# Windowed attention and two mixings on one core: one normalisation per attention tile, fourteen casts on GpSimd, another beginning and end

## The chip, the core and the metric

One NeuronCore of a Trainium2 chip runs one program. TensorE (PE) multiplies matrices, VectorE (DVE), ScalarE (ACT) and GpSimd (POOL) work on tiles of 128 partitions, SyncE (SP) issues nearly all DMAs. The metric is the device time of one execution in microseconds; smaller is better. Before the change it is 547.12 us, the median of 3 runs (547.0 to 549.04).

## The reference

```python
scores = scale * q @ k.T + bias            # 2 batches, 8 heads, 768 rows, head size 64
keep = is_global | is_local                # the first n_global columns, and a band of n_local
a = softmax(where(keep, scores, -1e9));  x = a @ v          # joined to [2, 768, 512]
xn = (x - mean) / sqrt(var + 1e-6) * g_ln
x = x + relu(xn @ w_ch1) @ w_ch2           # first mixing, 512 -> 2048 -> 512
u = x + (relu(x.T @ w_tok1) @ w_tok2).T    # token mixing, 768 -> 256 -> 768
out = u + relu(u @ moe2_w_ch1) @ moe2_w_ch2      # second mixing, 512 -> 1536 -> 512
```

The weights are float64 in DRAM and are read as 64-bit words. With these inputs n_global is 8 and n_local is 96, so a row tile of 128 attends to its own and the previous column tile.

## The kernel before, in words

The 1536 rows are 12 tiles T of 128. `window_tile` writes the attention of one tile: for two pairs of heads at a time the scores (L451, PE), the mask with the row maximum (L468, DVE), the exponential (L473, ACT), the transposed probabilities (L478, PE), their copy out of PSUM (L526 on ACT or L529 on DVE), the product with V (L483, PE), and at the end the division by the row sums (`scale`, L537 to L539, DVE). The product has a 65th column of ones, so the row sum comes out of the same matmul. Tiles 0 to 5 work in float32 this way; tiles 6 to 11 split the probabilities into two halves of 16 bits and transpose them on PE or by a DMA (the string `PT`).

`norm_ops` normalises a tile: statistics (L609 to L611, DVE), a power and two products (L618 to L621, POOL), the scaling (L624, ACT), the gain (L631, POOL), a high half (L587, ACT), a low half (L589, DVE or POOL), and a transposing DMA into `xa` or `xb` (L591, SP). Three tiles make a group; a mixing's first matmul needs all three.

`Weights.split` makes a weight block of 128 x 512 from a staged 512 KB load (`stg`, L166): a cast of the top words to float16 (`fw`, L755, ACT), a join with the shifted bits (`wf`, L761, DVE), the high half (L777, ACT), the low half (L780 POOL or L783 DVE). The first mixing has 16 blocks `a` and 16 blocks `b`. `mm3` (L372 to L374) multiplies halves in three products.

The program of each engine is written out by `Plan`: every step is an `Op` with an engine, a cost and a priority, and `order` picks, engine by engine, the ready step of the least priority whose buffers are free. The priorities come from the tables at the foot (`AHEAD`, `SLOT`, `LEADS` and others), the engine of many steps from strings of letters (`V` DVE, `G` POOL, `A` ACT). Between the steps of the beginning `emit` puts matmuls without use (`keep_busy`, L106), which keep PE's clock from falling.

PSUM is four pools of two banks: `m`, `s`, `t` and `k`. Before the change pool `t` holds both the transposed probabilities and the products with V (`PV`); pool `k` is used by `chain`, the accumulators of the mixings' paired products, from 236 us on.

`setup_consts` runs first: two tiny DMAs bring n_global and n_local to one partition (L50), DVE turns them into floats (L80, L83) and the flag that picks the fast path (L93 to L95), a matmul with a row of ones spreads the values over 128 partitions (L87), and a copy brings them out of PSUM (L97). Then the masks. At the end, tiles 10 and 11 are stored after the plan's other steps, both on SP (L1119), then every engine reads the flag `again` (L1437) and jumps over the general path (L1439).

Of the kernel before, what the change touches and what calls it, by code (L numbers as in the profile page):

```python
# [44 lines left out]
def setup_consts(o, tp):  # L45

    tc, nc, cp = o.tc, o.nc, o.cp
    w = tp.tile([1, 2, 2], I32, name="nwords")
    for i, n in enumerate((o.n_global, o.n_local)):
        (nc.sync, nc.scalar)[i].dma_start(w[:, i, :], n.bitcast(I32).rearrange("(o a) -> o a", o=1))  # L50
    for x in FIRST:
        if len(x) == 2:
            load(o, x[1], x[0])
        elif o.w64:
            load_words(o, o.stgs[len(o.staged)], x)
            o.staged.append(x)
# [3 lines left out]
    ones = tp.tile([1, P], F32, name="ones")  # L60
    nc.vector.memset(ones[:], 1.0)
    idle = o.nps.tile([P, 256], F32, name="idle")
    keep_busy(o, idle, BUSY[0])
# [12 lines left out]
    for fw in o.fws:  # L76
        nc.scalar.memzero(fw[:])

    neg = tp.tile([1, 2, 1], F32, name="neg")
    nc.vector.scalar_tensor_tensor(out=neg[:], in0=w[:, :, 0:1], scalar=0.0, in1=w[:, :, 1:2], op0=ALU.is_lt,  # L80
                                   op1=ALU.add)
    nval = tp.tile([1, 2, 1], F32, name="nval")
# [9 lines left out]
    ng, nl = nval[:, 0, :], nval[:, 1, :]  # L92
# [16 lines left out]
def distances(o, tp):  # L109


    nc = o.nc
    ri = tp.tile([P, 4 * P], I32, name="ri")
    ci = tp.tile([P, 1, NGF], I32, name="ci")
    rel = o.cp.tile([P, 4 * P], F32, name="rel")
    col = o.x[NTT - 2][:, :NGF].rearrange("p (o c) -> p o c", o=1)
    t = tp.tile([P, 4 * P], F32, name="mt")
# [7 lines left out]
    nc.vector.tensor_tensor(out=rel[:], in0=rel[:], in1=t[:], op=ALU.max)  # L125
    return rel, col
# [250 lines left out]
def bank(o, use, *dims):  # L377

    t = o.ps[BANKS[use]].tile([P, 512], F32, tag=BANKS[use], name=use)
# [20 lines left out]
def window_tile(o, plan, prio, T, slot):  # L400
# [33 lines left out]
    if T >= SPLIT:  # L434

        ao = Buf("ao", lambda: o.sm.tile([P, H, 2, D + 1], F32, tag="ao", name="ao", bufs=2))
        sm = Buf("sum", lambda: o.sm.tile([P, H], F32, tag="sum", name="sum", bufs=3))
    mn = Buf("mn", lambda: o.sm.tile([P, H], F32, tag="mn", name="mn", bufs=3))
    x = o.x[T][:].rearrange("p (h d) -> p h d", h=H)
    for p in range(4):  # L440
        k = k0 + p
        if p % 2 == 0:
# [12 lines left out]
            if T < SPLIT:  # L455
                bv = psum_buf(o, "PV", [4, D + 1])
# [4 lines left out]
        if T >= SPLIT:  # L461
            pt = Buf("ph", lambda: o.sm.tile([P, 8, P], F16, tag="ph", name="ph", bufs=o.sizes["ph"]))
            pq = Buf("pq", lambda: o.sm.tile([P, 8 * P], F16, tag="pq", name="pq", bufs=o.sizes["pq"]))
            bv = psum_buf(o, "PV", [2, 2, D + 1])
# [15 lines left out]
        def pv(p=p, pt=pt, bv=bv):  # L480
# [50 lines left out]
        if T < SPLIT:  # L531
            op("T", 2 * PVC * n, prio(k + slot["PV"]), pv, r=[(pt, 0), *vkeys], w=[(bv, p % 2)], get=[bv] if p % 2 == 0 else [])
        if T < SPLIT and p % 2 == 1:
            sm = Buf("sum", lambda: o.sm.tile([P, 4], F32, tag="sum", name="sum", bufs=3))

            def scale(p=p, bv=bv, sm=sm):
                nc.vector.tensor_scalar(out=sm.t[:], in0=bv.t[:, :, D], scalar1=1e-9, scalar2=None, op0=ALU.add)  # L537
                nc.vector.reciprocal(out=sm.t[:], in_=sm.t[:])
                nc.vector.tensor_tensor(out=x[:, 2 * p - 2:2 * p + 2], in0=bv.t[:, :, :D], in1=sm.t[:].rearrange(  # L539
                    "p (h o) -> p h o", o=1).to_broadcast([P, 4, D]), op=ALU.mult)  # L540

            op("V", 0.7, prio(k + slot["inv"]), scale, r=[(bv, 0), (bv, 1)], w=[("x", T, p // 2)], get=[sm])
# [101 lines left out]
class Guard:  # L644
# [7 lines left out]
    def __init__(self, o, plan):  # L652
# [7 lines left out]
        o.junk = o.gp.tile([P, 512], BF16, name="junk")  # L660
        for k, (a, b, lo, hi) in self.AT.items():
            for i, y in ((1, lo), (2, hi)):
                plan.op("G", 0.2, GUARD0, lambda i=i, a=a, b=b, y=y: nc.gpsimd.memset(c[:, i, a:b], y), w=[("lim", k, i)])
        for i, y in enumerate((1.0, TINY)):
            plan.op("G", 0.2, GUARD0, lambda i=i, y=y: nc.gpsimd.memset(o.ones[:, i:i + 1], y), w=[("one", i)])
# [48 lines left out]
class Weights:  # L714
# [26 lines left out]
    def split(self, src, prio, dst, key, get=(), r=(), after=()):  # L741
# [360 lines left out]
PVE = 'VAAAAV'  # L1102
EVX = 'AAAAVVAAVAVA'
QKC, PVC = 0.266, 0.224
SLOT = {'gk': -109.0, 'exp': 30.58, 'T': -47.76, 'PV': -30.42, 'inv': 2.16, 'st': 2.77, 'xn': 23.42, 'tr': 35.01}
NACT = range(0, 4)
START = {"V": 1.1, "A": 1.5, "G": 3.5, "S": 9.0}
# [3 lines left out]
BANKS = {'L1': 'm', 'L2': 'm', 'L2S': 't', 'norm': 'k', 'chain': 'k', 'uT': 't', 'S': 's', 'T': 't', 'PV': 't', 'tok1': 's', 'tok2': 't'}  # L1111
# [5 lines left out]
def store(o, T):  # L1117
    b, t = divmod(T, NT)
    o.nc.sync.dma_start(o.out[b, t * P:(t + 1) * P, :], o.x[T][:])  # L1119


def rest_pools(o, ctx):
# [15 lines left out]
    o.ps = {p: pool("ps" + p, o.sizes[p], space=PSUM) for p in PSUMS}  # L1138
# [3 lines left out]
def rest(o, ctx, attn, fast):  # L1142
# [136 lines left out]
LEADS, FLEAD = 25.19, 159.37  # L1279
F2LEAD = [-28.4, -27.06]  # L1280
FE, SE = 'VGVVVVGVVGVG', 'GVGGVVVV'
HEAD = 56.45
DUE = [32.72, 16.66, 78.81, 48.03]
EARLY = [42.85, -26.35, 1.23, -4.64]
LEAD = -178.69
EVAC = 20.66
TOK1 = 41.8
TOKW, TOK0 = 247.08, 102.37
# [5 lines left out]
class WindowAttention:  # L1294
# [8 lines left out]
    def ops(self, o, plan, prio):  # L1303
# [3 lines left out]
        plan.op("G", 0.3, 20.0, lambda: nc.gpsimd.memset(o.vb[:, :, :, 0, D:], VSC), w=[("vb", z, 0) for z in range(3)])  # L1307
        plan.op("G", 0.5, 20.0, lambda: nc.gpsimd.memset(o.vb[:, :, :, 1, D:], 0.0), w=[("vb", z, 1) for z in range(3)])
        plan.op("V", 1.25, HEAD0 + 8.0, lambda: may(o, o.bmt, o.col, o.x[NTT - 1][:, :3 * P], 0, 3, False), r=[("first", 1, 1)], w=[("rel",)], lock=True)
# [17 lines left out]
class GeneralAttention:  # L1327
# [7 lines left out]
    def attend(self, o, ctx):  # L1335
# [16 lines left out]
        for T in range(NTT):  # L1352
# [24 lines left out]
            for h in range(H):  # L1377
# [16 lines left out]
                acc = bank(o, "PV", 512)  # L1394
# [15 lines left out]
def mixer_kernel(ctx, tc, q, k, v, n_global, n_local, g_ln, w1, w2, wt1, wt2, w3, w4, out):  # L1410
# [20 lines left out]
    near = nc.values_load(flag[0:1, 0:1], min_val=0, max_val=1)  # L1431
# [5 lines left out]
    again = nc.values_load(o.again[0:1, 0:1], min_val=0, max_val=1)  # L1437
# [50 lines left out]
```

## Time and profile before

| | before |
|---|---|
| median of 3 runs | 547.12 us |
| the profiled execution's own time | 546.87 us |
| its span, first to last instruction | 545.1 us |
| mean granted TensorE clock | 0.996 of 2.4 GHz |
| PE, DVE, ACT, POOL busy | 532.0, 408.6, 337.1, 163.2 us |
| DMA moved | 89.81 MB, 57.2% of 16 engines' span |

Some 1.8 us of an execution lie outside the span. A busy PE counts matmuls without use too, and matmuls overlap, so the question is not how busy PE is but when its needed work may start and where it then stops.

### The profile page before, as it was taken

The page shows a single profiled execution, that of the slowest core. Times are in us where ns is not written, and L with a number is a line of the kernel's source. Part 1 is how long each engine was busy: PE and PEld are TensorE (multiplying, and loading weights), DVE is VectorE, ACT ScalarE, POOL GpSimd, SP SyncE. Part 2 cuts the span into 40 slices and gives each one's busy share as a digit, 9 for nine tenths or more (in the row PEclk, how much of TensorE's full clock was granted, in tenths as well). Part 3 has the DMA queues.
Part 4 walks back from the last instruction along what each step waited for, and adds up shares of the span by engine and source line. Part 5 has one row for each costly group of instructions (what it writes and reads, how often), then busy time and mean ns, then how long its engine had stood idle before and what let it go on. Part 6 is the DMA issues. An engine that isn't in the chain of part 4 may idle for free.

```text
span 545.1 us, 9103 instructions
## 1 busy us (share of the span) xinstructions
PE 532.0 (98%) x3132; PEld 299.7 (55%) x3132; DVE 408.6 (75%) x902; ACT 337.1 (62%) x760; POOL 163.2 (30%) x181
## 2 busy tenths in 40 slices
PE   7989999999999999999999999999999999999995
PEld 5866666666555555555555555455445545555542
DVE  6977998788699632788897898988987786655341
ACT  6988668786976433459948766576685545524210
POOL 2133221223132424253444245324343442220000
PEclk9998999999999999999999999999999999999999
DMA  8898977695998568277319793146745332302012
GB/s 242 267 232 238 294 209 182 202 259 164 208 234 237 207 174 231 97 240 244 97 39 192 186 267 110 40 136 210 268 121 158 92 133 68 113 1 78 2 40 82
DMA packets 99242, 89.81 MB, mean 165 GB/s; under 512 B 58484, under 2 KB 72820, under 8 KB 99188
## 3 DMA queue, kind: packets, MB, share of 16 engines
q1 hardware_dynamic: 99186, 89.15, 57.2%
q8 instruction: 26, 0.43, 0.3%
q14 instruction: 28, 0.23, 0.1%
q10 hardware_dynamic: 2, 0.00, 0.0%
HBM read 61.87 MB, written 17.83 MB: 146 GB/s over the span
## 4 chain that ended last, share of the span: by engine, by line
PE 84%; ACT 6%; DVE 4%; DMA 2%; SPq 1%; issue 1%; POOL 0%; ACTq 0%
PE L L372 11%; PE L L374 11%; PE L L373 11%; PE L2S L372 9%; PE L2S L374 9%; PE L2S L373 9%; PE chain L372 4%; PE chain L374 4%; PE chain L373 4%; PE S L451 3%; DMA stg<-in_moe_w_ch_dram 2%; PE tok L373 2%; PE tok L372 2%; PE tok L374 2%; ACT ex L473 2%; PE T L478 2%
## 5 line engine op out<-in xcount | busy, mean ns | idle before, releaser
L372 PE MATMUL L2S<-wb,h 128*128 128x512 f16 x228 | 86.4, 379 | 0.0
L373 PE MATMUL L2S<-wb,h 128*128 128x512 f16 x228 | 86.4, 379 | 0.0
L374 PE MATMUL L2S<-wb,h 128*128 128x512 f16 x228 | 86.4, 379 | 0.0
L900 DVE SCALAR_TENSOR_TENSOR x<-L2S,x 128x512 f32<-128x512 f32 x57 | 39.2, 688 | 43.0 <-PE L2S L374 42.9
L755 ACT ACTIVATE fw<-stg 128x512 f16<-128x512 bf16 x62 | 47.5, 777 | 20.1 <-DMA stg<-in_moe_w_ch_dram 16.2
L374 PEld LDWEIGHTS <-h 128*128 128x128 f16 x336 | 32.9, 98 | 39.6
L372 PEld LDWEIGHTS <-h 128*128 128x128 f16 x336 | 33.1, 98 | 35.7
L373 PEld LDWEIGHTS <-h 128*128 128x128 f16 x336 | 32.9, 98 | 35.8
L834 POOL TENSOR_TENSOR Q<-wa 128x512 f32<-128x512 f16 x18 | 25.6, 1422 | 74.8 <-DVE sz L834 55.2
L473 ACT ACTIVATE ex<-ex,mn 128x256 f32<-128x256 f32 (+1 forms) x96 | 41.3, 480 | 7.5 <-DVE mn L468 7.4
L761 DVE SCALAR_TENSOR_TENSOR wf<-stg,fw 128x512 uint32<-128x512 uint32 x62 | 45.0, 739 | 0.5 <-ACT fw L755 0.5
L834 POOL TENSOR_TENSOR Q<-Q 128x256 f32<-128x256 f32 x36 | 31.5, 874 | 32.6 <-DVE Q L834 31.2
L372 PE MATMUL L<-wb,h 128*128 128x512 f16 x108 | 40.9, 379 | 0.0
L373 PE MATMUL L<-wb,h 128*128 128x512 f16 x108 | 40.9, 379 | 0.0
L374 PE MATMUL L<-wb,h 128*128 128x512 f16 x108 | 40.9, 379 | 0.0
L372 PEld LDWEIGHTS <-wa 128*128 128x128 f16 x268 | 26.2, 98 | 20.4 <-issue 2.7
L374 PEld LDWEIGHTS <-wa 128*128 128x128 f16 x268 | 26.2, 98 | 17.3
L373 PEld LDWEIGHTS <-wa 128*128 128x128 f16 x268 | 26.2, 98 | 17.3
L364 DVE SCALAR_TENSOR_TENSOR h<-L,h 128x384 f16<-128x384 f32 x40 | 22.1, 553 | 17.4 <-ACT h L358 17.1
L372 PE MATMUL L<-xa,wa 128*128 128x384 f16 x104 | 34.0, 327 | 0.0
L373 PE MATMUL L<-xa,wa 128*128 128x384 f16 x104 | 33.9, 326 | 0.0
L374 PE MATMUL L<-xa,wa 128*128 128x384 f16 x104 | 33.9, 326 | 0.0
(235 smaller groups left out, 1341.2 us busy)
## 6 DMA issues: line engine op xcount, KB each, us to landing
stg<-in_moe_w_ch_dram SPq DMA_DIRECT2D x56, 512.0 KB, 5.5
wa<-scr_1a SPq DMA_DIRECT2D x24, 256.0 KB, 3.5
wb<-scr_1b SPq DMA_DIRECT2D x24, 256.0 KB, 3.6
scr_1a<-wa SPq DMA_DIRECT2D x16, 256.0 KB, 4.0
scr_1b<-wb SPq DMA_DIRECT2D x16, 256.0 KB, 3.8
K<-in_k_dram SPq DMA_DIRECT2D x12, 256.0 KB, 3.6
Q<-in_q_dram SPq DMA_DIRECT2D x12, 256.0 KB, 4.3
V<-in_v_dram SPq DMA_DIRECT2D x12, 256.0 KB, 4.3
```

Source lines behind the costliest of these rows:

```text
L364: nc.vector.scalar_tensor_tensor(out=lo(), in0=src(), scalar=0.0, in1=plain(hi()), op0=ALU.max, op1=ALU.subtract)
L372: nc.tensor.matmul(ps, ah, bh, start=first, stop=False, **k)
L373: nc.tensor.matmul(ps, ah, bl, start=False, stop=False, **k)
L374: nc.tensor.matmul(ps, al, bh, start=False, stop=last, **k)
L451: nc.tensor.matmul(bs[j].t[:, i, :w], o.Q[r, qs, p + i, :], o.K[r, slots, p + i, :], start=True, stop=True)
L473: nc.scalar.activation(out=ex.t[:, j, :w], in_=ex.t[:, j, :w], func=AF.Exp, bias=mn.t[:, h:h + 1], scale=-1.0)
L478: nc.tensor.transpose(bt.t[:, j, i, :], ex.t[:, j, i * P:(i + 1) * P], o.ident[:])
L755: op("A", 0.66, prio - 2, lambda: nc.scalar.activation(out=fw.t[:, :, 1], in_=stg.t[:, 4:2049:4].bitcast(BF16), func=AF.Copy, scale=2.0 if ...
L761: op("V", 0.6, prio - 1, lambda: nc.vector.scalar_tensor_tensor(out=raw().bitcast(U32), in0=stg.t.bitcast(U32)[:, 1:1024:2], scalar=13, in ...
L834: op(eng, {"G": 0.1 + n * 0.00227, "V": 0.07 + n * 0.00104}[eng], prio, lambda: e.tensor_tensor(out=out(), in0=a(), in1=b(), op=alu), lock ...
L900: n = op("V", 0.6, prio, lambda: nc.vector.scalar_tensor_tensor(out=x[:], in0=b.t[:], scalar=BACK if o.half else 1.0, in1=x[:], op0=ALU.mu ...
```

## The change

What it does, part by part:

- The division by the row sums of tiles 0 to 5 runs once per tile on 512 columns, instead of once per half tile on 256. The products with V of one tile fill both banks of pool `k` (one tile `k2`, whose banks `bank` hands out in turn); `PV2` in pool `t` stays for tiles 6 to 11.
- 14 of the 32 casts `fw` of the first mixing run on POOL as a multiplication by a constant (`FA1`, `FB1`).
- n_global and n_local are brought to all 128 partitions by the DMAs themselves; the row of ones, the matmul and the copy go. Half of one mask step (three column blocks of four) moves behind the first tile's masks (`distant`).
- The values that `values_load` reads are no longer checked against bounds at run time.
- Tile 10 is stored before the last addition is issued, and tile 11 by ACT's queue.
- All tables are set anew, so each engine's order is another one throughout. Among them: `PVE`, `EVX`, `PT` (9 of 24 pairs of tiles 6 to 11 transposed on PE instead of 12), `LOB1` (5 more low halves on DVE), `FE` and `SE`.

```diff
-    w = tp.tile([1, 2, 2], I32, name="nwords")
+    w = tp.tile([P, 2, 2], I32, name="nwords")
...
-        (nc.sync, nc.scalar)[i].dma_start(w[:, i, :], n.bitcast(I32).rearrange("(o a) -> o a", o=1))
+        (nc.sync, nc.scalar)[i].dma_start(w[:, i, :], n.bitcast(I32).rearrange("(o a) -> o a", o=1).partition_broadcast(P).rearrange("p o a -> p (o a)"))
...
-    ps = o.nps.tile([P, 2], F32, name="nps")
-    nc.tensor.matmul(ps[:], ones[:], nval[:, :, 0], start=True, stop=True)
-    keep_busy(o, idle, BUSY[1])
...
-    t = o.ps[BANKS[use]].tile([P, 512], F32, tag=BANKS[use], name=use)
+    t = o.k2[:, next(o.kb)] if BANKS[use] == "k" else o.ps[BANKS[use]].tile([P, 512], F32, tag=BANKS[use], name=use)
...
+            def scale(sm=sm):
+                v = o.k2[:, :, :4 * (D + 1)].rearrange("p b (h d) -> p b h d", h=4)
+                nc.vector.tensor_scalar(out=sm.t[:], in0=v[:, :, :, D:], scalar1=1e-9, scalar2=None, op0=ALU.add)
                 nc.vector.reciprocal(out=sm.t[:], in_=sm.t[:])
+                nc.vector.tensor_tensor(out=x.rearrange("p (b h) d -> p b h d", b=2), in0=v[:, :, :, :D], in1=sm.t[:].to_broadcast([P, 2, 4, D]),
+                                        op=ALU.mult)
...
+            if o.half and src[0] == 1 and (FA1 if src[1] == "a" else FB1)[src[2]] == "G":
+                op("G", 0.95, prio - 2, lambda: nc.gpsimd.tensor_scalar(
+                    out=fw.t[:, :, 1], in0=top(), scalar1=2.0 if wide else 1.0, scalar2=None, op0=ALU.mult),
+                   r=[(stg, 0), ("zeros",)], w=[(fw, 0)], get=[fw])
...
+        store(o, BEHIND[0])
         for x in rest:
             x.fn()
-        for T in BEHIND:
-            store(o, T)
+        store(o, BEHIND[1], "scalar")
...
-    near = nc.values_load(flag[0:1, 0:1], min_val=0, max_val=1)
+    near = nc.values_load(flag[0:1, 0:1], min_val=0, max_val=1, skip_runtime_bounds_check_because="a product of comparisons, 0 or 1")
...
+FA1 = 'GGAGAAAAGGAAAGAG'
+FB1 = 'GAGAGAGAGAAGAGAA'
```

How the order moves shows best at three places. The first is PE around the first matmul of the first mixing (`L<-xa,wa`), before:

```order
L483 MATMUL PV<-V,pt 128x65 x8
L478 MATMUL T<-ident,ex 128x128 x4
L451 MATMUL S<-K,Q 128x256 x4
L478 MATMUL T<-ident,ex 128x128 x4
L483 MATMUL PV<-V,pt 128x65 x8
L478 MATMUL T<-ident,ex 128x128 x4
L372 LDWEIGHTS wa
```

and now:

```order
L470 MATMUL T<-ident,ex 128x128 x8
L445 MATMUL S<-K,Q 128x256 x4
L475 MATMUL k_211<-V,pt 128x65 x8
L470 MATMUL T<-ident,ex 128x128 x4
L445 MATMUL S<-K,Q 128x256 x4
L470 MATMUL T<-ident,ex 128x128 x4
L365 LDWEIGHTS wa
```

The last product with V of tile 4's first half now stands behind that point instead of ahead of it: 68 transposes and 64 products are ahead of it before, 64 and 56 now, while the scores ahead of it are the same 40. In the whole program there are 8 transposes fewer.

The second place is ACT around the scaling and the high half of tile 2 (`xn<-x_66` and the `xh` behind it), the last step on ACT that the first mixing's `xa` waits for, before:

```order
L777 ACTIVATE wb<-wf 128x512
L755 ACTIVATE fw_63<-stg_203 128x512
L624 ACTIVATE xn<-x_66,st 128x512
L473 ACTIVATE ex<-ex,mn 128x256 x4
L526 ACTIVATE pt<-T 128x512
L587 ACTIVATE xh<-xn 128x512
```

and now:

```order
L757 ACTIVATE fw_62<-stg 128x512
L465 ACTIVATE ex<-ex,mn 128x256
L617 ACTIVATE xn<-x_66,st 128x512
L465 ACTIVATE ex<-ex,mn 128x256 x3
L580 ACTIVATE xh<-xn 128x512
```

Between the program's start and the exponentials that the first mixing's matmul stands behind, ACT has 11 casts `fw`, 12 copies `pt` of 512 columns and 3 high halves `wb` before, and 3, 9 and none now.

The third place is POOL in the same stretch, behind the memsets of the beginning, now:

```order
L753 TENSOR_SCALAR fw_63<-stg 128x512
L611 TENSOR_TENSOR st<-st,minus 128x1
L613 TENSOR_TENSOR st<-st,minus 128x1
L614 TENSOR_TENSOR st<-st 128x1
L753 TENSOR_SCALAR fw_62<-stg_189 128x512
L624 TENSOR_TENSOR xn<-xn,gB 128x512
L582 TENSOR_TENSOR xh<-xn,xh 128x512
```

The casts stand between the small steps and the gain of the normalisation, which run on POOL in both kernels: one that waits for its load holds back a tile's `xn`.

## Rows read from the trace of the kernel before

**Rows 1.** The page's first part: busy time, share and instructions of each engine.

```profile
PE 532.0 (98%) x3132; PEld 299.7 (55%) x3132; DVE 408.6 (75%) x902; ACT 337.1 (62%) x760; POOL 163.2 (30%) x181
```

**Rows 2.** Stretches of time: from:to, length, busy us by engine, clock, DMA share, GB/s.

```profile
10.00:20.00 10.00, 8.41 (x71) 6.94 (x71) 6.94 (x34) 9.40 (x28) 1.27 (x3) 1.00 0.96 289
...
40.00:60.00 20.00, 18.67 (x132) 14.49 (x131) 15.64 (x43) 15.06 (x31) 6.94 (x8) 0.91 0.93 249
60.00:100.00 40.00, 39.88 (x271) 24.88 (x268) 35.21 (x107) 30.45 (x76) 7.21 (x7) 1.00 0.81 231
```

**Rows 3.** Timeline of PE, 51 to 72 us: start, length, instruction, idle before and releaser.

```profile
52.41 0.84 PE L478 MATMUL T<-ident,ex 128*128 128x128 f32 x4 [0.48 <-ACT ex L473]
53.08 0.33 PE L372 MATMUL L<-xa,wa 128*128 128x384 f16 x1
```

**Rows 4.** Groups on ACT by form, 7.3 to 52.9 us: busy, mean ns, idle before.

```profile
L755 ACT ACTIVATE fw<-stg 128x512 f16<-128x512 bf16 x11 | 8.4, 774 | 3.3 <-DMA stg<-in_moe_w_ch_dram 3.3
L526 ACT ACTIVATE pt<-T 128x512 f32<-128x512 f32 x12 | 7.0, 581 | 0.7 <-PE T L478 0.6
...
L777 ACT ACTIVATE wb<-wf 128x512 f16<-128x512 f32 x3 | 1.8, 623 | 0.0
```

**Rows 5.** Groups on DVE by form, 6.8 to 52.9 us: the division by the sums.

```profile
L539 DVE TENSOR_TENSOR x<-PV,sum 128x256 f32<-128x256 f32 x9 | 3.8, 424 | 0.3
...
L538 DVE RECIPROCAL sum<-sum 128x4 f32<-128x4 f32 x9 | 1.6, 178 | 0.3
L537 DVE TENSOR_SCALAR sum<-PV 128x4 f32<-128x4 f32 x9 | 1.4, 161 | 6.5 <-PE PV L483 6.5
```

**Rows 6.** Timeline, 34 to 60 us: tile 2's normalisation after its statistics.

```profile
38.75 0.19 POOL L621 TENSOR_TENSOR st<-st 128x1 f32<-128x1 f32 x1
...
40.61 0.79 ACT L624 ACTIVATE xn<-x,st 128x512 f32<-128x512 f32 x1
...
43.56 0.62 ACT L587 ACTIVATE xh<-xn 128x512 f16<-128x512 f32 x1
...
46.04 0.69 DVE L589 TENSOR_TENSOR xh<-xn,xh 128x512 f16<-128x512 f32 x1
...
48.07 1.28 SPq L591 DMA_TRANSPOSE xa<-xh  x1
```

**Rows 7.** The chain of waits, 33 to 54 us: start, length, instruction.

```profile
34.24 1.11 PE PV L483 x8
35.34 0.44 PE T L478 x4
```

**Rows 8.** Groups on POOL by form, whole program.

```profile
L834 POOL TENSOR_TENSOR Q<-wa 128x512 f32<-128x512 f16 x18 | 25.6, 1422 | 74.8 <-DVE sz L834 55.2 <-DVE wa L783 19.6
...
masks.py:199 POOL TENSOR_SCALAR_AFFINE_SELECT ident<-ident 128x128 f32<-128x128 f32 x1 | 0.3, 348 | 0.1
```

**Rows 9.** Lines L761 and L783 by themselves: ns min/median/max, first and last start.

```profile
L761 DVE SCALAR_TENSOR_TENSOR wf<-stg,fw x62: 651/683/1576, 18.1 to 399.2; 128x512 uint32<-128x512 uint32 x62
...
L783 DVE SCALAR_TENSOR_TENSOR wb<-wf,wb x12: 674/684/1566, 55.3 to 412.2; 128x512 f16<-128x512 f32 x12
```

**Rows 10.** The end: timeline, then lines L1437 and L1439 by themselves (durations in ns).

```profile
538.77 0.69 DVE L900 SCALAR_TENSOR_TENSOR x<-L2S,x 128x512 f32<-128x512 f32 x1 [1.90 <-PE L2S L374]
539.49 0.33 SPq L1119 DMA_DIRECT2D out_dram<-x  x1
...
L1437 SPq TENSOR_LOAD <-flags x1: 441/441/441, 540.5 to 540.5; - x1
L1437 SPq FUSED_REGOPS  x1: 182/182/182, 543.4 to 543.4; - x1
L1437 SPq SEQ_ASSERT  x1: 28/28/28, 543.7 to 543.7; - x1
...
L1439 SPq EVENT_SEMAPHORE  x8: 17/17/17, 542.8 to 543.4; - x8
```

**Rows 11.** Timeline, 0 to 30 us: the copy that the change removes.

```profile
4.30 0.16 DVE L97 COPY both<-nps 128x2 f32<-128x2 f32 x1
```

More of the change, by code (lines that the diff above doesn't have):

```diff
@@ L59, in setup_consts @@
     nc.vector.memset(o.zero, 0.0)
-    ones = tp.tile([1, P], F32, name="ones")
-    nc.vector.memset(ones[:], 1.0)
     idle = o.nps.tile([P, 256], F32, name="idle")
-    keep_busy(o, idle, BUSY[0])
+    keep_busy(o, idle, BUSY)
     rel, col = distances(o, tp)
@@ L437, in window_tile @@
         sm = Buf("sum", lambda: o.sm.tile([P, H], F32, tag="sum", name="sum", bufs=3))
+    bvs = [psum_buf(o, "PV", [4, D + 1]) for _ in range(2)] if T < SPLIT else None
     mn = Buf("mn", lambda: o.sm.tile([P, H], F32, tag="mn", name="mn", bufs=3))
@@ L531, in window_tile @@
         if T < SPLIT:
[L532 to L537, printed above, removed]
+            op("T", 2 * PVC * n, prio(k + slot["PV"]), pv, r=[(pt, 0), *vkeys], w=[(bvs[p // 2], p % 2)], get=bvs if p == 0 else [])
+        if T < SPLIT and p == 3:
+            sm = Buf("sum", lambda: o.sm.tile([P, 2, 4, 1], F32, tag="sum", name="sum", bufs=3))
+            def scale(sm=sm):
+                v = o.k2[:, :, :4 * (D + 1)].rearrange("p b (h d) -> p b h d", h=4)
+                nc.vector.tensor_scalar(out=sm.t[:], in0=v[:, :, :, D:], scalar1=1e-9, scalar2=None, op0=ALU.add)
                 nc.vector.reciprocal(out=sm.t[:], in_=sm.t[:])
-                nc.vector.tensor_tensor(out=x[:, 2 * p - 2:2 * p + 2], in0=bv.t[:, :, :D], in1=sm.t[:].rearrange(
-                    "p (h o) -> p h o", o=1).to_broadcast([P, 4, D]), op=ALU.mult)
-            op("V", 0.7, prio(k + slot["inv"]), scale, r=[(bv, 0), (bv, 1)], w=[("x", T, p // 2)], get=[sm])
+                nc.vector.tensor_tensor(out=x.rearrange("p (b h) d -> p b h d", b=2), in0=v[:, :, :, :D], in1=sm.t[:].to_broadcast([P, 2, 4, D]),
+                                        op=ALU.mult)
+            op("V", 0.95, prio(k + slot["inv"]), scale, r=[(b, i) for b in bvs for i in range(2)], w=xk(T), get=[sm])
         if p == 3 and 0 < t < NT - 1:
@@ L660, in __init__, with begin @@
         o.junk = o.gp.tile([P, 512], BF16, name="junk")
+    def begin(self):
+        o, plan, nc, c = self.o, self.plan, self.o.nc, self.o.check
         for k, (a, b, lo, hi) in self.AT.items():
             for i, y in ((1, lo), (2, hi)):
[L663 removed]
+                plan.op("G", 0.05, GUARD0, lambda i=i, a=a, b=b, y=y: nc.gpsimd.memset(c[:, i, a:b], y), r=[("first", 3, 1)], w=[("lim", k, i)])
         for i, y in enumerate((1.0, TINY)):
[L665 removed]
+            plan.op("G", 0.05, GUARD0, lambda i=i, y=y: nc.gpsimd.memset(o.ones[:, i:i + 1], y), r=[("first", 3, 1)], w=[("one", i)])
         plan.op("A", 0.3, GUARD0, lambda: nc.scalar.activation(out=o.half1[:, 0:2], in_=o.ones[:], func=AF.Copy), r=[("one", 0), ("one", 1)], w=[("half", 0)])
@@ L1114, with store @@
 SIZES = {**WIDE, 'hid': 12, 'wa': 8, 'wb': 8, 'wf': 4, 'fw': 3, 'stg': 4, 'xn': 2, 'ph': 3, 'pq': 2, 'xh': 2, 'uh': 2, 'xz': 3, 'sz': 4}
-def store(o, T):
+def store(o, T, queue="sync"):
     b, t = divmod(T, NT)
-    o.nc.sync.dma_start(o.out[b, t * P:(t + 1) * P, :], o.x[T][:])
+    getattr(o.nc, queue).dma_start(o.out[b, t * P:(t + 1) * P, :], o.x[T][:])
 def rest_pools(o, ctx):
@@ L1137, in rest_pools @@
     o.gp = pool("gp")
-    o.ps = {p: pool("ps" + p, o.sizes[p], space=PSUM) for p in PSUMS}
+    o.ps = {p: pool("ps" + p, 1 if p == "k" else o.sizes[p], space=PSUM) for p in PSUMS}
+    o.k2, o.kb = o.ps["k"].tile([P, 2, 512], F32, name="k2"), cycle((0, 1))
     o.kept = {}
@@ L1306, in ops, with distant @@
         window_tile(o, plan, lambda k: HEAD0 + k, 0, dict.fromkeys(SLOT, 0.0))
-        plan.op("G", 0.3, 20.0, lambda: nc.gpsimd.memset(o.vb[:, :, :, 0, D:], VSC), w=[("vb", z, 0) for z in range(3)])
-        plan.op("G", 0.5, 20.0, lambda: nc.gpsimd.memset(o.vb[:, :, :, 1, D:], 0.0), w=[("vb", z, 1) for z in range(3)])
-        plan.op("V", 1.25, HEAD0 + 8.0, lambda: may(o, o.bmt, o.col, o.x[NTT - 1][:, :3 * P], 0, 3, False), r=[("first", 1, 1)], w=[("rel",)], lock=True)
+        o.guard.begin()
+        plan.op("G", 0.1, 20.0, lambda: nc.gpsimd.memset(o.vb[:, :, :, 0, D:], VSC), r=[("first", 3, 1)], w=[("vb", z, 0) for z in range(3)])
+        plan.op("G", 0.1, 20.0, lambda: nc.gpsimd.memset(o.vb[:, :, :, 1, D:], 0.0), r=[("first", 3, 1)], w=[("vb", z, 1) for z in range(3)])
+        def distant():
+            sl = slice(0, 3 * P)
+            nc.vector.tensor_tensor(out=o.bmt[:, sl], in0=o.bmt[:, sl], in1=o.x[NTT - 4][:, sl], op=ALU.max)
+            may(o, o.bmt, o.col, o.x[NTT - 1][:, sl], 0, 3, False)
+        plan.op("V", 1.7, HEAD0 + 8.0, distant, r=[("first", 1, 1)], w=[("rel",)], lock=True)
         for (d, e, at), engs in zip(((0, 2, HEAD0 + 8.1), (2, 3, MASK2)), (MK1, MK2)):
```

89 lines of the change are left out of this document (43 added, 46 removed).

## The prediction

> **What bounds the kernel now.** I read the page's first part, then a table of stretches, then the timeline of PE where the first mixing starts, then the groups of ACT and DVE ahead of that point, and last the end of the program. PE is busy 98% of the span [rows 1], and from 60 to 100 us 39.88 of 40 [rows 2]: once the first mixing has begun at 53.08 [rows 3], PE has no idle time that counts, up to the last matmul. So the kernel is three pieces: 53.1 us until the first mixing's first matmul, a stretch as long as PE's needed work, and an end that begins when the last addition starts at 538.77 [rows 10]. A change gains only where it brings 53.08 forward, takes work from PE behind it, or shortens the end; what it takes from ACT or DVE later is free time.
>
> Ahead of 53.08 PE waits for others. The reader is to see in [rows 3] that the last transposes before it waited 0.48 us for an exponential on ACT, and in [rows 2] that ACT is busy 9.40 of 10 us already from 10 to 20, while DMA stands at a share of 0.93 to 0.96. DVE in the same time has gaps: 6.5 us of them ahead of the division, waiting for products with V on PE [rows 5], which in turn wait for copies on ACT. ACT is the first bound there, the DMA feed the second.
>
> **The beginning, ACT's part.** Eight casts leave ACT ahead of that point (11 to 3), at 774 ns [rows 4]: 6.2 us. Three copies `pt` fewer at 581 ns are 1.7, three high halves `wb` at 623 ns are 1.9 [rows 4]. Together 9.8 us. Neighbours on ACT overlap (the rows of a group are longer than the distance from one start to the next), so I count some 85%: 8.3 us. With nothing else in the way the transposes at 52.41 come at 44.1, and the first mixing with them.
>
> **The beginning, the normalisation of tile 2.** Its steps lose time in queues: the small step ends at 38.94 and `xn` begins at 40.61; `xh` ends at 44.18 and its low half begins on DVE at 46.04; that ends at 46.73 and the DMA is issued at 48.07 [rows 6]. That is 1.7 + 1.9 + 1.3 = 4.9 us behind other work. Now no cast and no `wb` stands between them, and the low half moves to POOL. DVE gains a little too: a tile's division costs 2 x (161 + 178 + 424) = 1526 ns before; now the last step is twice as wide, at most 2 x 424, so 1187 or less [rows 5], a saving of 0.34 us a tile or more, three tiles ahead of the point. Against it, one product with V must now wait for the division of the tile before, since both banks are one tile's.
>
> **The beginning, the feed.** On SP, 11 loads of 512 KB stand ahead of tile 2's transposing DMA before, 9 now, and one store of 256 KB more: 0.79 MB fewer, which at the 249 GB/s of 40 to 60 us [rows 2] is 3.2 us. If the DMA engines alone set the pace, the DMA comes 3.2 us earlier and the first matmul at 49.9. The truth lies between 44.1 and 49.9; the DMA share is not 1, and the queues above were engines' queues, so I take the middle, 47.0: **6.1 us earlier**. The few operations at the very start (a copy of 0.16 us [rows 11], a memset, a narrower mask step) are inside that number; the DMA to 128 partitions may land later than that to one, which no row shows, and I let the two cancel.
>
> **Work that moves behind the point.** Four transposes fewer are done ahead of it and eight fewer in all, so 4 fewer remain, 0.44 us; eight products with V are put off, 1.11 us [rows 7]. Net +0.67 us.
>
> **The price of a cast on POOL.** No row shows one with this form. The bounds are a two-input operation on 512 columns, 1422 ns, and a one-input operation on a quarter of that, 348 ns [rows 8]; I take 1.0 us, nearer the former, since 512 columns are moved. 14 casts add 14 us to an engine that is busy 30% [rows 1], so the sum is touched only through what stands behind a cast. The Trainium skill (GPSIMD Engine Reference, section 4.1, Engine selection) would put elementwise work on VectorE, but calls one-input work on GpSimd roughly line-rate; by the best case of its section 3.1 a cast would be an estimated 0.77 us, and the sum would stay as it is.
>
> **The end.** SP issues the last store at 539.49 for 0.33 us, reads the flag from 540.5, waits on eight semaphores from 542.8 to 543.4, and then runs the bounds check until 543.7 [rows 10]. Now ACT issues that store and SP has gone ahead to those waits, so ACT's own walk (issue, load, jump) sets the end; at SP's pace it arrives at 542.8, and the eight waits and the check behind it go: 543.7 - 542.8 = **0.9 us**. The lower bound is the check alone, 182 ns; the upper is that the second store's issue and jump cost nothing, some 1.9.
>
> **The stretch between.** PE's order there is written anew, and the loads, low halves and additions must now come some 6 us earlier too. From 60 to 100 us DVE is busy 35.21 of 40 and DMA 0.81 [rows 2], and five more low halves fall to DVE at 684 ns [rows 9], 3.4 us. Bounds: nothing lost, or 3 us of waits on PE. I take 1.0.
>
> **Sum.** -6.1 + 0.67 - 0.9 + 1.0 = -5.3; 546.87 - 5.3 = 541.6 us, against the profiled execution's own 546.87, which is 0.25 below the median 547.12. A measurement of this kernel can tell about 0.5% from no change, 2.7 us. So the forecast is faster.
>
> **Rivals.**
> *The feed holds* (0.17). ACT is free but `xa` comes with the DMA: first matmul at 49.9, waits of 1.5 us behind it: -3.2 + 0.67 - 0.9 + 1.5 = -1.9, 545.0. For it: the DMA share of 0.93 to 0.96 [rows 2]. Against it: only 3.3 of ACT's idle time was put down to loads [rows 4].
> *The relief is not passed on* (0.08). The casts leave ACT, but DVE's order or the shared banks keep the attention at its pace; only 1 us of the first piece goes: -1.0 + 0.67 - 0.9 = -1.2, 545.7. The change would not do what its casts are there for. Against it: the 0.48 us wait for ACT [rows 3].
> *All of it* (0.15). First matmul at 44.1 and no wait later: -9.0 + 0.67 - 0.9 = -9.2, 537.6.
> *Slower: POOL holds DVE* (0.07). `wf` takes 651 ns at the least and 1576 at the most, `wb` 674 and 1566 [rows 9]: beside a POOL operation a DVE operation can be held for up to 0.9 us. The Trainium skill (SBUF - State Buffer, section "SBUF: two separate sides") tells of a port pair that DVE and GpSimd lock for a whole instruction; the two longest rows agree with it, and it speaks against moving a cast from ACT, which has its own port, to POOL. By that mechanism the five casts ahead of the first mixing cost 5 x 0.9 = 4.5 us of DVE time and undo most of the gain; behind it DVE has 40 - 35.2 = 4.8 us free up to 100 us [rows 2] and would get nine more holds, 8.1, and the low halves, 3.4: 8.1 + 3.4 - 4.8 = 6.7 us of waits on PE. -6.1 + 4.5 + 6.7 + 0.67 - 0.9 = +4.9, 551.8. It decides once the holds and the added low halves together pass those 4.8 us. Against it: the medians, 683 and 684, stand 10 to 32 ns over the least, so holds are rare although POOL is busy 30%, and 14 casts raise that little.
>
> **How the numbers follow.** The forecast has 0.53. Faster by over 0.5% means below 544.4: nearly all of the forecast (0.52), all of "all of it", and half of the feed's case, 0.09, since its waits may be nothing: 0.76. Within 0.5% falls the rest but for the held DVE: 0.16. Slower by over 0.5%: 0.07 and a little for a stall in the new order that nothing here shows, 0.08. The range, 537.0 to 546.0, takes in the forecast from both ends of the first piece, the feed's case and the unpassed relief; it leaves out the slower case, the tail of "all of it", and the upper ends of the two cases near 545.
>
> **What would show it.** In the profile after: the first `L<-xa,wa` matmul near 47 and not near 53 (ACT's or the feed's pace by whether the transposing DMA or an exponential comes last ahead of it); ACT's busy share from 10 to 40 us falling by some 5 us; casts on POOL near 1.0 us; PE without idle time from there on; the span's end some 5.4 us after the last addition's start instead of 6.3. It would be wrong if the first matmul stays above 50, if PE shows gaps of more than 3 us behind it, or if `wf` and `wb` on DVE grow by over 0.1 us in the mean.

## The result and the profile after

The changed kernel takes 551.56 us in the median (549.89 to 556.8, 20 runs), the kernel before 547.83 in the runs beside it. The ratio is 1.0069 with a 95% interval of 1.0051 to 1.0087: slower by 0.7%, where 541.6 us and 1% faster were forecast. The profiled execution took 549.89 us, of which the span is 548.0 (before 546.87 and 545.1). It is the fastest of the twenty, so its lines show the change at its best.

PE's timeline gives the start and the first mixing (columns: start, length, instruction, idle before it and its releaser):

```profile
8.56 1.23 PE L445 MATMUL S<-K,Q 64*128 64x128 f32 x8 [4.57 <-DVE x L142]
...
51.26 0.33 PE L365 MATMUL L<-xa,wa 128*128 128x384 f16 x1
```

The same of before has its first scores at 5.05 and the first mixing at 53.08 [rows 3]:

```profile
5.05 1.23 PE L451 MATMUL S<-K,Q 64*128 64x128 f32 x8
```

So the change starts 3.5 us later, and the stretch from the first scores to the first mixing is 5.3 us shorter (42.70 for 48.03); 1.8 us are left. Even this is not to be counted on: in the run of the change with eight casts more at its end, whose engines do the same steps in the same order up to there, the first mixing starts 0.9 us later than before:

```profile
8.85 1.22 PE L445 MATMUL S<-K,Q 64*128 64x128 f32 x8 [4.86 <-DVE x L142]
...
54.01 0.33 PE L365 MATMUL L<-xa,wa 128*128 128x384 f16 x1
```

DVE's timeline tells why it starts late:

```profile
6.79 0.16 DVE L78 SCALAR_TENSOR_TENSOR neg<-nwords 128x2 f32<-128x2 int32 x1 [3.82 <-DMA nwords<-in_n_global_dram]
```

In before that row stands at 3.30 without a wait. Not only the numbers are late. In the table of stretches (from:to, length, busy PE, PEld, DVE, ACT, POOL, clock, DMA share, GB/s) the whole feed of before runs at 193 to 356 GB/s from 2 us on:

```profile
2.00:3.00 1.00, 1.00 (x7) 0.64 (x5) 0.96 (x4) 0.99 (x3) 0.69 (x5) 1.00 0.80 193
3.00:4.00 1.00, 0.69 (x4) 0.32 (x2) 0.88 (x5) 0.82 (x2) 0.00 (x0) 1.00 1.11 356
4.00:5.00 1.00, 1.00 (x5) 0.46 (x4) 0.77 (x4) 0.00 (x0) 0.12 (x3) 1.00 0.88 252
```

In the change next to nothing moves until 5 us, though the loads of K and Q are issued from 1.18 on:

```profile
2.00:3.00 1.00, 1.00 (x7) 0.69 (x6) 0.94 (x4) 0.99 (x3) 0.68 (x5) 1.00 0.04 1
3.00:4.00 1.00, 1.00 (x5) 0.39 (x3) 0.00 (x0) 0.69 (x2) 0.00 (x0) 1.00 0.16 9
4.00:5.00 1.00, 0.00 (x0) 0.00 (x0) 0.00 (x0) 0.00 (x0) 0.00 (x0) 1.00 0.41 89
```

The list of PE's waits from 100 us on, empty before, now reads (total us, times, longest):

```profile
PE k L365 <- DVE h L357: 2.1, 4, 0.7
PE k L365 <- ACT junk L678: 1.2, 1, 1.2
PE k L365 <- DVE V L961: 0.2, 1, 0.2
```

These 3.5 us all stand at matmuls into `k`, the tile that now holds both banks of the chain. The end (the last addition, then the last store, on ACT's queue) answers to [rows 10]:

```profile
543.08 0.69 DVE L901 SCALAR_TENSOR_TENSOR x<-L2S,x 128x512 f32<-128x512 f32 x1 [1.90 <-PE L2S L367]
543.80 0.37 ACTq L1122 DMA_DIRECT2D out_dram<-x  x1
```

From the last addition's start to the end of the span it is 548.0 - 543.08 = 4.92 us, before 6.33. The casts on GpSimd are one row (count, busy us, mean ns):

```profile
L753 POOL TENSOR_SCALAR fw<-stg 128x512 f16<-128x512 bf16 x14 | 25.3, 1815 | 27.0 <-DVE rel L140 9.6
```

### The profile page after: what moved, and what is told of

It is laid out like the page before. It is cut to its first block, busy times and chain, and to the rows that moved or that the text cites. A ratio compares the mean times of both kernels' runs of the same rounds, so it can differ in the third digit from the quotient of the medians.

```text
span 548.0 us, 9018 instructions
## 1 busy us (share of the span) xinstructions
PE 530.5 (97%) x3115; PEld 297.5 (54%) x3115; DVE 417.8 (76%) x897; ACT 329.9 (60%) x746; POOL 174.3 (32%) x181
## 4 chain that ended last, share of the span: by engine, by line
PE 88%; DVE 4%; DMA 3%; ACT 3%; issue 1%; SPq 0%; ACTq 0%; DVEq 0%
PE L L365 12%; PE L L367 12%; PE L L366 12%; PE L2S L367 9%; PE L2S L366 9%; PE L2S L365 9%; PE k L365 4%; PE k L367 4%; PE k L366 4%; PE S L445 4%; PE k L475 2%; PE T L470 2%; PE tok L367 2%; PE tok L366 2%; PE tok L365 2%; DMA nwords<-in_n_global_dram 1%
## 5 line engine op out<-in xcount | busy, mean ns | idle before, releaser
L835 POOL TENSOR_TENSOR Q<-Q 128x256 f32<-128x256 f32 x18 | 17.8, 987 | 92.1 <-DVE Q L835 92.1
L757 ACT ACTIVATE fw<-stg 128x512 f16<-128x512 bf16 x48 | 37.0, 777 | 11.1 <-DMA stg<-in_moe_w_ch_dram 7.6
L351 ACT ACTIVATE h<-L 128x384 f16<-128x384 f32 x40 | 19.4, 485 | 27.2 <-PE L L367 27.0
L753 POOL TENSOR_SCALAR fw<-stg 128x512 f16<-128x512 bf16 x14 | 25.3, 1815 | 27.0 <-DVE rel L140 9.6
```

The costliest lines, as they stand in the source:

```text
L351: nc.scalar.activation(out=hi(), in_=src(), func=AF.Relu if relu else AF.Copy)
L753: op("G", 0.95, prio - 2, lambda: nc.gpsimd.tensor_scalar(out=fw.t[:, :, 1], in0=top(), scalar1=2.0 if wide else 1.0, scalar2=None, op0=AL ...
L757: op("A", 0.66, prio - 2, lambda: nc.scalar.activation(out=fw.t[:, :, 1], in_=top(), func=AF.Copy, scale=2.0 if wide else 1.0), r=[(stg, 0 ...
L835: op(eng, {"G": 0.1 + n * 0.00227, "V": 0.07 + n * 0.00104}[eng], prio, lambda: e.tensor_tensor(out=out(), in0=a(), in1=b(), op=alu), lock ...
```

## The experiments

Two suspects came out of that comparison: the copy of the two numbers to 128 partitions, and the chain's two banks as one tile.

### The copy, alone in the kernel before

```
-    w = tp.tile([1, 2, 2], I32, name="nwords")
+    w = tp.tile([P, 2, 2], I32, name="nwords")
...
-    nc.tensor.matmul(ps[:], ones[:], nval[:, :, 0], start=True, stop=True)
```

> The kernel before with one part of the change alone: the two numbers copied to 128 partitions, no spreading matmul and no copy behind it. Theory (late landing, loads behind held up): first score op later by 2 to 3.5 us than before's 6.90, the time 1.5 to 3.5 us over the kernel before's. Rival (it only looks late in the change because other work there starts late): first score op within 1 us of 6.90 and the time within 0.7 us of the kernel before's.

Measured: 551.06 us, ratio 1.0055 (1.0026 to 1.0084). The first score op starts at 10.06 (before 6.90), PE waits 4.82 us ahead of its first scores. The theory holds: this one part costs about 3 us.

### The copy undone in the change

```
-    w = tp.tile([P, 2, 2], I32, name="nwords")
+    w = tp.tile([1, 2, 2], I32, name="nwords")
...
+    nc.tensor.matmul(ps[:], ones[:], nval[:, :, 0], start=True, stop=True)
```

> The change with one part undone: the two numbers go to one partition again and are spread by a 1x2 matmul, as in the kernel before; tables, casts, banks and end stay. Theory (the copy to 128 partitions lands late and holds the loads behind it): the first score op of VectorE is back near 7 us (9.79 in the change, 6.90 before), K and Q land near 4.6 us instead of 6.5, and the time falls by 2.5 to 3.5 us against the change, to some 548 to 549. Rival (the start is hidden, because the first weights' casts and loads set when the first mixing begins): first score op near 7, but the first mixing matmul stays near 51 us and the time within 1 us of the change's.

Measured: 546.83 us, ratio 0.9999 (0.9967 to 1.0031). The first score op is at 6.04, K lands 4.4 us and Q 5.1 us after its issue, and the first mixing begins at 47.48, not near 51. So the start is not hidden, and the time falls by more than the 2.5 to 3.5 us expected. The waits at `k` stay at 3.5 us.

### Both copies on ScalarE's queue

```
-        (nc.sync, nc.scalar)[i].dma_start(w[:, i, :], n...
+        nc.scalar.dma_start(w[:, i, :], n...
```

> The change with both copies of the numbers to 128 partitions issued on ScalarE's queue, so that the loads of K and Q stand first on SyncE's. Theory (a copy to 128 partitions keeps only its own queue busy): K and Q land at 4.4 to 5 us as in the kernel before, the numbers still near 5.5 to 6.5, the first score op of VectorE stays near 9.5 to 10 because it waits for the numbers. Rival (it slows the engines that all queues share): K and Q land at 6 us or later all the same.

A single execution: K and Q land 5.7 us after their issue, between what the theory (4.4 to 5) and the rival (6 or later) said; the first score op is at 9.12. The stretches show a feed that starts and is then stopped:

```profile
2.00:3.00 1.00, 1.00 (x7) 0.67 (x6) 0.94 (x4) 0.99 (x2) 0.68 (x5) 1.00 0.38 99
3.00:4.00 1.00, 1.00 (x5) 0.38 (x3) 0.00 (x0) 1.00 (x3) 0.00 (x0) 1.00 0.45 160
4.00:5.00 1.00, 0.00 (x0) 0.00 (x0) 0.00 (x0) 0.17 (x1) 0.00 (x0) 1.00 0.12 15
```

So in this execution the copies hold up loads on another queue too, if less than those behind them on their own (6.2 and 6.4 us in the change). That agrees with the Trainium skill (DMA: Bandwidth & Descriptors, section "Issuing engines are not separate DMA queues"), by which transfers of all queues share the same engines. Why 2 KB keep them from moving data for so long, no run here shows.

### The chain's banks as two tiles

```
-    o.k2, o.kb = o.ps["k"].tile([P, 2, 512], F32, name="k2"), cycle((0, 1))
+    o.k2, o.kb = [o.ps["k"].tile([P, 512], F32, name=f"k2{i}") for i in range(2)], cycle((0, 1))
...
-                nc.vector.tensor_scalar(out=sm.t[:], in0=v[:, :, :, D:], scalar1=1e-9, ...
+                for i in range(2):
+                    nc.vector.tensor_scalar(out=sm.t[:, i], in0=v[i][:, :, D:], scalar1=1e-9, ...
```

> The change with the two banks of the chain as two tiles instead of one tile with two halves; the division then takes five VectorE instructions per tile instead of three. Order of the tensor engine unchanged. Theory (in one tile each chain waits for the eviction of the chain ahead of it in the other half): the 3.5 us in which TensorE waits at the chains' matmuls behind 100 us shrink to under 1 us, and the time falls by 2 to 3.5 us against the change, to 548 to 549.5. Rival (the waits come from the order in the new tables, ScalarE and VectorE being late with their own work): the waits stay over 2.5 us and the time within 1 us of the change's.

Measured: 546.62 us, ratio 0.9995 (0.9966 to 1.0025). From 100 us on PE's list of waits is empty. The order of PE's work is that of the change; only what a chain's matmul waits for differs. The same three rows of PE's order, in the change and with two tiles:

```
L365 MATMUL k_211<-fx_187,sz 128x384 [waits DVE_49]
L365 MATMUL k_211<-xa,wa 128x384 [waits DVE_49]
L365 MATMUL k_211<-t_2838,sz 128x384 [waits DVE_49]

L365 MATMUL k_212<-fx_187,sz 128x384 [waits Activation_49]
L365 MATMUL k_212<-xa,wa 128x384
L365 MATMUL k_212<-t_2851,sz 128x384 [waits Activation_49]
```

In one tile a chain waits until VectorE has read the chain ahead of it in the other half, though they share no number. In the profiled execution the first mixing starts at 53.05, later than in the change's, and the time falls all the same, in the median by more than the 2 to 3.5 us expected.

### Both mendings together

The edits are those of the copy undone and of the two tiles, in one kernel.

> The change with both mendings together: the two numbers to one partition and the spreading matmul, and the chain's banks as two tiles. Theory (late copy and shared tile are separate costs of 4.7 and 4.9 us by the two single runs): both come off, 551.56 - 4.7 - 4.9 = 541.9, so 541 to 543.5; by the trace no wait of TensorE at a chain over 0.5 us behind 100 us, first score op near 6 us. Rival (the two overlap, since what is gained early is lost at another wait): 545 to 547.

Measured: 542.08 us, ratio 0.9910 (0.9882 to 0.9938): the two costs add up, and this version is faster than the change and than the kernel before. It is called the mended version below.

```profile
47.67 0.33 PE L372 MATMUL L<-xa,wa 128*128 128x384 f16 x1
...
535.43 0.69 DVE L909 SCALAR_TENSOR_TENSOR x<-L2S,x 128x512 f32<-128x512 f32 x1 [1.90 <-PE L2S L374]
```

### What a cast on GpSimd costs by itself

```
+        for i, (y, x) in enumerate(((wide, few), (wide, all_), (tight, few), (tight, all_)) * 2):
+            op("G", 1.8, prio, lambda x=x, y=y: nc.gpsimd.tensor_scalar(out=y, in0=x, scalar1=1.0, ...
```

> The change with eight casts of 128x512 bf16 to f16 more on GpSimd near the end, behind 500 us, where GpSimd has nothing else and VectorE is a third busy: two each of strided into strided (as the 14 of the change), dense into strided, strided into dense, dense into dense. They write nothing that is used. If the 1.7 us of the 14 casts come from VectorE's work beside them, the strided ones take under 1.2 us here. If they come from the strides, strided into strided stays near 1.7 and dense into dense is under 1.2. If from the conversion itself, all four take 1.6 or more.

A single execution. By line, with durations in ns as min/median/max (strided input `stg`, dense input `junk`), then the timeline:

```profile
L694 POOL TENSOR_SCALAR fw<-stg x4: 1529/1616/2117, 497.5 to 516.6; 128x512 f16<-128x512 bf16 x4
L694 POOL TENSOR_SCALAR fw<-junk x4: 1487/1558/1635, 508.6 to 518.2; 128x512 f16<-128x512 bf16 x4
```

```profile
516.57 1.56 POOL L694 TENSOR_SCALAR fw<-stg 128x512 f16<-128x512 bf16 x1
518.22 1.49 POOL L694 TENSOR_SCALAR fw<-junk 128x512 f16<-128x512 bf16 x1
```

Dense or strided, with VectorE half busy (4.45 of 9 us from 509 to 518), it takes 1.49 to 1.67 us, at the 1.6 I had named; only the first took 2.12. So the strides do not make the 1.7 to 1.8 us, and less work beside it takes little off; a cast with VectorE idle throughout was not run. The Trainium skill's best case (GPSIMD Engine Reference, section 3.1), from which 0.77 us was estimated, is half of what is measured; the measurement decides.

### The end alone, in the kernel before

```
+        store(o, BEHIND[0])
         for x in rest:
             x.fn()
-        for T in BEHIND:
-            store(o, T)
+        store(o, BEHIND[1], "scalar")
```

> The kernel before with the end of the change alone: the store of tile 10 ahead of the last addition, that of tile 11 on ScalarE's queue, and no bounds check on the two flags. Theory (the end gains what the traces show, 6.33 against 4.92 us from the last addition's start to the end of the span): this stretch is 4.7 to 5.3 us and the time 0.9 to 1.6 us under the kernel before's. Rival (the gain of the end came from the new order ahead of it): the stretch stays over 5.8 us, the time within 0.5 us.

Measured: 546.27 us, ratio 0.9975 (0.9946 to 1.0004); from the last addition at 538.77 to the end of 544.5 it is 5.7 us, 0.6 less than before and between the two expectations. The same end takes 4.92 in the change and 540.6 - 535.43 = 5.17 in the mended version. SyncE's last wait for the store stands at 542.9, 3.4 us behind its issue at 539.50; in the change at 546.4, 2.6 us behind 543.80. So the end gained between 0.6 and 1.4 us, the less the longer the last store took.

### The casts, and orders planned anew

These runs change the plan, so that the order on all engines changes with the edit.

```
-FA1 = 'GGAGAAAAGGAAAGAG'
+FA1 = 'A' * 16
-FB1 = 'GAGAGAGAGAAGAGAA'
+FB1 = 'A' * 16
```

> The change with all 32 casts of the first mixing on ScalarE again, everything else as in the change. Theory (the casts at 1.7 us each on GpSimd cost little on the path, because the stretch ahead of the first mixing got 4.7 us shorter with them): the first mixing matmul moves later by 1 to 4 us from 51.26, and the time rises by 0.5 to 3 us over the change. Rival (the slow casts hold VectorE and the weights up): the first mixing matmul comes earlier and the time falls by 1 us or more. If neither: within 0.7 us, the casts are off the path.

Measured: 561.28 us, ratio 1.0240 (1.0197 to 1.0283); first mixing at 63.28. The direction is the theory's, the size more than three times it; TensorE's granted clock is 0.63 from 40 to 60 us and 0.50, the level of 1.2 GHz, from 44 to 52. The same edit in the mended version:

> The mended version (542.08 us) with all 32 casts on ScalarE. It tells what the move of 14 casts brings once the start isn't late. By the prediction's step (casts, copies and high halves leave ScalarE ahead of the first mixing) the first mixing matmul goes from 47.67 to 53 or later and the time to 546 to 550; in the change itself the same edit cost 9.7 us, with TensorE's granted clock at 0.63 from 40 to 60 us. Rival (the move of the casts is no part of the gain, the new order is): within 1.5 us of 542.08.

552.98 us, ratio 1.0104 (1.0061 to 1.0147), first mixing at 57.07, and the clock 0.70 from 40 to 60 us: the direction of the prediction's step, but 3 us beyond the range expected. And the other way round, the casts alone in the kernel before, with the change's `FA1` and `FB1`:

> The kernel before with the 14 casts on GpSimd alone, its own tables and start and end. By the prediction's step ScalarE is relieved ahead of the first mixing, its first matmul comes at 48 to 51 instead of 53.08 and the time falls by 2 to 5 us under the kernel before's. Rival (the slow casts, 1.7 us against 0.77, hold up the weights and what is behind them on GpSimd, and without an order made for them nothing is gained): first mixing matmul at 52.5 or later and the time within 1 us of the kernel before's or above it.

551.96 us, ratio 1.0067 (1.0034 to 1.0100). The first mixing comes at 49.73, 3.35 us earlier, in the direction of the prediction's step; the time rises where a fall of 2 to 5 us was expected. Behind that point the kernel gives back 7.0 us: from there to the last addition it takes 492.71 us (before 485.69). PE is idle for 4.0 of it, and 2.3 us more of transposes and products with V stand there than before, put off by the new order. The longest two of PE's waits are for low halves of weights:

```profile
PE L L374 <- DVE wa L788: 1.8, 1, 1.8
PE L L373 <- DVE wb L788: 1.0, 1, 1.0
```

and in the timeline around the first of them:

```profile
87.11 1.69 DVE L788 SCALAR_TENSOR_TENSOR wa<-wf,wa 128x512 f16<-128x512 f32 x1
...
87.09 1.16 POOL L785 TENSOR_TENSOR wb<-wf,wb 128x512 f16<-128x512 f32 x1 [6.09 <-ACT wb L782]
```

The `wa` for which PE waits is held on DVE beside an operation on POOL: 1.69 us where the median is 0.68. So the rival "POOL holds DVE" is real, but by a low half that was on POOL before, and here by one hold. In this order the relief on ACT was given back behind the point; whether another order would have kept it, no run here shows.

The division by half rows in the mended version:

```
-        if T < SPLIT and p == 3:
+        if T < SPLIT and p % 2 == 1:
...
-                for i in range(2):
-                    nc.vector.tensor_tensor(out=x[:, 4 * i:4 * i + 4], in0=v[i][:, :, :D], ...
+                nc.vector.tensor_tensor(out=x[:, 2 * p - 2:2 * p + 2], in0=bv.t[:, :, :D], ...
```

> The mended version (numbers to one partition, chain banks as two tiles; 542.08 us) with the division of the first tiles by half rows again, behind the second and the fourth pair of heads, as in the kernel before; the planner orders the work anew by the same tables. Theory (the form of the division is off the path, its stages being bound by ScalarE, the loads and TensorE): first mixing matmul within 1.5 us of the mended version's 47.67 and the time within 1.5 us. Rival (one division per tile brings a part of the gain, since VectorE has up to 0.5 us a tile less to do): first mixing matmul 2 us or more later and the time up by 2 us or more.

Measured: 549.5 us, ratio 1.0030 (1.0001 to 1.0058), first mixing at 58.15. My theory, that the form is off the path, missed by 10 us there; but the order changed with the form, the clock is 0.50 to 0.83 from 40 to 60 us, and the profiled execution took 552.48 us, 3 us over its median.

And the planner's cost of a GpSimd cast at its true size in the mended version:

```
-                op("G", 0.95, prio - 2, lambda: nc.gpsimd.tensor_scalar(
+                op("G", 1.7, prio - 2, lambda: nc.gpsimd.tensor_scalar(
```

> The mended version (542.08 us) with one number of the planner changed: it counts a cast on GpSimd as 1.7 us, which is what the trace shows, instead of 0.95. If the order suffers from the wrong price, the waits ahead of the first mixing shrink and the time falls by 0.5 to 2 us, to 540 to 541.5. Rival (the tables were fitted to the chip with the wrong price in them, so any other order is worse or as good): 541.5 to 545.

Measured: 551.48 us, ratio 1.0066 (1.0041 to 1.0090); first mixing at 49.35, then 493.98 us to the last addition for the mended version's 487.76. The truer price did not help, and the time is worse by far than the rival's 545. That fits tables that were fitted with the wrong price, but one other order does not show it.

Is it the clock? Three of these again, with matmuls of zeros in PE's planned gaps and the real work in the same order:

```
-        end, until = 0.0, self.TICK * self.WARM[1] - self.ORIGIN
+        end, until = 0.0, self.TICK * (17 if self.WARM[1] else 0) - self.ORIGIN
```

> The division by half rows in the mended version (549.5 us), with 17 matmuls of zeros more in TensorE's planned gaps between some 22 and 53 us, the real work in the same order. Theory (its 7.4 us over the mended version are the clock: a granted clock of 0.50 to 0.83 from 40 to 60 us is 8.5 us of full-speed time lost): the clock stays over 0.9 there, the first mixing matmul comes by 51 us and the time falls by 4 us or more, to 541.5 to 545.5. Rival (the clock fell because the work was late already, and the edit makes it late): the fillers change the clock but the time stays within 2 us of 549.5.

> All casts on ScalarE in the mended version (552.98 us), with 30 matmuls of zeros more in TensorE's planned gaps. Theory (6.8 us of its 10.9 us over the mended version are the clock, the other 4 the casts): the clock stays over 0.9 from 36 to 60 us and the time is 545 to 548. Rival (the casts on ScalarE hold up the work by the whole of it): within 2 us of 552.98.

> The order planned with 1.7 us for a cast on GpSimd (551.48 us), with 30 matmuls of zeros more in TensorE's planned gaps. Theory (6.8 us of its 9.4 us are the clock): the clock stays over 0.9 and the time is 543 to 547. Rival: within 2 us of 551.48.

Measured: 550.8 us for 549.5, 551.21 for 552.98, 550.06 for 551.48, all within 2 us as the rivals had it. The third is the clear one. Its stretches (PE busy, clock, DMA share, GB/s) without the fillers

```profile
36.00:40.00 4.00, 4.00 (x18) 0.50 0.83 193
40.00:44.00 4.00, 4.00 (x20) 0.50 0.85 226
44.00:48.00 4.00, 4.00 (x30) 0.80 0.34 66
```

and with them

```profile
36.00:40.00 4.00, 3.52 (x27) 1.00 0.89 272
40.00:44.00 4.00, 3.19 (x26) 1.00 1.00 256
44.00:48.00 4.00, 4.00 (x34) 1.00 0.42 83
```

The clock is kept, PE is idle instead, the first mixing stays at 49.36 for 49.35, and the time falls by 1.4 us at most, since the two intervals overlap (1.0005 to 1.0061 and 1.0041 to 1.0090). There PE was waiting for others, and a slower clock mostly filled the wait. With all casts on ScalarE the fillers kept the clock at 1.00 from 36 to 48 us (0.50 from 40 to 48 without), and only 1.8 of the 10.9 us went; behind 48 it fell there too. In the run on halves the fillers did not keep the clock (0.50 from 44 to 52), so its share stays open, and with it what the division's form costs by itself.

## Why the prediction was wrong

The steps, against the profiled spans (before 545.1, change 548.0, mended version 540.6), in us:

| step | predicted | change | mended |
|---|---|---|---|
| first mixing, from 53.08 | -6.1 | -1.82 | -5.41 |
| work put off behind it | +0.67 | +0.98 | +1.06 |
| PE idle behind it (before 0.15) | +1.0 | +3.54 | +0.20 |
| PE busy in no group counted | 0 | +1.61 | +0.81 |
| end | -0.9 | -1.41 | -1.16 |
| sum | -5.3 | +2.9 | -4.5 |

The medians stand 3.7 us apart (551.56 and 547.83): the column of the change is that of its fastest execution. Two of the prediction's three signs of being wrong came, a first mixing above 50 and gaps of over 3 us behind it.

**The step that failed** is half a sentence: "the DMA to 128 partitions may land later than that to one, which no row shows, and I let the two cancel". It should have had bounds of its own. The copy costs 3.5 us at the first scores, holds the loads behind it, and by the runs with it alone and without it some 3 to 4 us of time (ratio 1.0055 in before; 1.0069 to 0.9999 in the change). Taking the copy out, like putting it in, left the order of all other steps as it was on every engine.

**The second is the stall term.** The prediction saw that "both banks are one tile's", and drew from it only one wait of a product with V. The same tile serves the chains from 236 to 525 us, where PE has no slack. That is 3.5 us of waits, and 1.0069 to 0.9995 in time.

**What was right.** With both out of the way the first mixing comes at 47.67 where 47.0 was forecast, the end gains about what it should, and the time is 542.08 where 541.6 was. `wf` and `wb` hardly grew: the mean of `wf` went from 739 to 752 ns and that of `wb` from 786 to 807, where the rival's sign was over 100 more, so the slower rival was not what happened. That it names 551.8 and 551.56 was measured is luck.

**What was luck in the 47.0.** It was the middle of two paces, ACT's and the feed's, and the runs confirm neither. PE's last wait ahead of the first mixing is for an exponential in the change and for a row maximum on DVE in the mended version, in neither for the transposing DMA:

```profile
48.52 0.44 PE L470 MATMUL T<-ident,ex 128*128 128x128 f32 x2 [0.71 <-ACT ex L465]
```

```profile
46.12 1.13 PE L452 MATMUL S<-K,Q 64*128 64x256 f32 x6 [0.24 <-DVE mn L467]
```

And ACT's busy time from 10 to 40 us fell by 2.65 us in the change (27.82 to 25.17) and by 1.27 in the mended version (to 26.55), not by 5. The clock is not what made the difference: before has 0.91 from 40 to 60 us [rows 2] and the mended version 1.00, but the run with only the copy undone has 0.95 there, 0.73 from 40 to 44, and starts the mixing at 47.48.

**What was mis-sized.** A cast on POOL is 1.7 to 1.8 us in the change and 1.5 to 1.7 with POOL to itself, outside the bounds of 0.35 to 1.42. They came from a two-input operation as if more inputs must be dearer. The sum held no term for it.

**What stays open.** How much of the 5.4 us belongs to the casts, the division and the order: each run that took one of them out also got another order, and lost 7 to 11 us. And the 0.8 to 1.6 us of PE's busy time that no group shows.

## What to carry to other kernels

Cost every edit of the first few microseconds with a row of its own: a transfer of a few bytes to every partition is no small thing when the first loads stand behind it, and one to a single partition with a small matmul behind it was some 3 us cheaper here. Two buffers that are used in turn should be two tiles: in one tile with two halves a use here waited for the reader of the other half, and the loss showed where the engine has no slack, far from the edit. Where a planner's tables were fitted for one order, take out single edits that leave the order alone first; a run with the order planned anew measures the order as well.

## What the runs showed of the hardware

The granted clock did not follow the length of an idle stretch alone. With the chain's banks as two tiles PE waits 4.84 us ahead of its first scores; with the eight casts added it does the same steps in the same order and waits 4.86 us. The first wait reads

```profile
8.84 1.23 PE L445 MATMUL S<-K,Q 64*128 64x128 f32 x8 [4.84 <-DVE x L142]
```

and the second stands with the result above. From 8 to 12 us (length, PE busy, clock, DMA share, GB/s) the first has the clock 1.00, the second 0.50, the level of 1.2 GHz:

```profile
8.00:12.00 4.00, 3.16 (x18) 1.00 1.12 277
```

```profile
8.00:12.00 4.00, 3.15 (x18) 0.50 1.09 276
```

The change itself (4.57 us of waiting) kept 1.00, the kernel before with the copy (4.82) had 0.50.

In the mended version PE is busy 2.68 of 4 us from 36 to 40 and the clock stays at 1.00; on halves it is busy 2.59 from 40 to 44, and the clock falls to 0.50 for the 12 us behind that. And a one-input cast of 512 columns on GpSimd (1.56 us) took longer than a two-input subtraction of as many (1.24 to 1.34 for `sz` and `wb` in the change).
